# Loading batch 0's values for the global softmax behind the twelfth fetch of w_out, not behind the thirteenth

## The chip, the cores and the metric

The kernel runs on one core of a Trainium2 chip. The metric is the time of one execution on the device, in microseconds (us), as a median of runs. The profile is of one further execution, recorded by the hardware profiler.

## The reference, cut to what is computed

Local and global attention, then a dense feed-forward layer, then a soft mixture of experts, all in f32; `w_in` and `w_out` arrive as 64-bit integers.

```
x = attention(q_l, k_l, v_l, q_g, k_g, v_g)   # 4 batches x 8 heads; 512 local rows
                                              # (window +-32, and 32 global keys) and 32 global
                                              # rows that see all 544 keys and values
x = x.transpose(...).reshape(2176, 512)
h = x @ w_in;  g = max(0.01*h, h);  y = g @ w_out             # 512 -> 2048 -> 512
logits = y @ phi                                              # 32 slots, 8 experts x 4
slot_input = softmax(logits, over rows).T @ y
slot_out[e] = max(slot_input[e] @ w1[e], 0) @ w2[e]
out = softmax(logits, over slots) @ slot_out
```

## The kernel before

**Stages.** One core does all four batches. The first 60 us or so are the local attention of batch 0, in four pairs of heads: transposes of q and k (`a_T`, L390), scores of 32-row blocks against a window of 128 keys (`a_S`, tile `sc`, L434, with a maximum on VectorE at L446 and exponentials on ScalarE at L454), transposes of the weights (`a_E`, tile `etp`, L473), products with the values (`a_V`, tile `po`, L493). From then on the attention of a later batch is interleaved with the feed-forward layer of finished 128-row tiles: `b_X` (transpose of x, tile `xtp`, L659), `b_H` (x @ w_in in twelve matmuls of 128x512 for a 512-wide slice, tile `hp`, L689), `b_L` (transpose of g, `gtp`, L726) and the logits. The last 90 us are the experts, with two rounds of weights w1 and w2 (tile `ew`), and the output (`sop` L1297, `sp` L1307, `op` L1321, evicted at L1340 and stored at L1343).

**w_out.** `p_items` turns w_out into f32 while batch 0's rows go through `b_H`. A 128-row piece is fetched (`fetch`, L233), converted by two ScalarE passes (L250, L251), two VectorE passes (L253, L257) and one GpSimd pass (L261), stored to DRAM as `wo_f` for later (L338), transposed on TensorE (tile `wotp`, L345), evicted on ScalarE (tile `wt`, L347) and multiplied with phi (`prod`, tile `ptps`, L354). There are 20 fetches. `begin` issues the first twelve: eight half pieces into buffers borrowed from the attention (tiles `sraw`, `eraw`, `kraw`), then four whole pieces (tile `rraw`) that fill the ring of four buffers. The other eight follow one by one, each as a ring buffer is used up. `fetch` keeps its last DMA in `raw_last[0]`.

**The values for the global softmax.** The 32 global rows of a batch see all keys and values, so `g_V` (tile `gpo`, L579) needs the values of the whole batch at once: `load_vn(0)` loads them, 1 MB into the tile `vn` (L206) and 64 KB into `vg` (L211). Its only caller for batch 0 stands after twelve items of `p_items` have been run, of which the tenth half or whole piece has caused the thirteenth fetch. `tc.issue_after(ins)` puts the instructions of its block, on `ins`'s engine, behind `ins` in that engine's order; it adds no wait on `ins`'s completion.

**Order.** The program gives the items in order, but a list scheduler lays out each engine's instruction stream from them with modelled times and from priorities; on the chip each engine then runs its stream in that fixed order. All DMAs of this stretch are issued from SyncE's queue (SP) in its order: fetches, stores of `wo_f`, q and k of batch 1 (L162, tiles `qn`, `kn`), the values of batch 1's windows (tile `vw`: two loads L177 and one L180 into 32 partitions, then two copies L184 and one L185 that spread them over the other partitions).

Of the kernel before, what the change touches and what calls it, by code (L numbers as in the profile page):

```python
# [20 lines left out]
def kernel(  # L21
# [181 lines left out]
    def load_vn(b):  # L203
        t = sa.tile([P, NW + 2, 2, D], F32, tag="vw", name="vn", bufs=2)
        t = t.rearrange("p a c d -> p (a c d)").rearrange("p (h t d) -> p h t d", t=NT, h=H)
        nc.sync.dma_start(  # L206
            out=t.rearrange("p h t d -> p h (t d)"),
            in_=v_l[b].rearrange("h (p t) d -> p h (t d)", t=NT),
        )
        g = sa.tile([SG, H, D], F32, tag="vg", name="vg", bufs=1)  # L210
        nc.sync.dma_start(out=g, in_=v_g[b].rearrange("h k d -> k h d"))  # L211
        vnat[b] = (t, g)
# [13 lines left out]
    raw_last = [None]  # L226
# [89 lines left out]
    def p_items():  # L316
# [7 lines left out]
        def begin():  # L324
            with tc.issue_after(raw_last[0]):
                wout_s.spread([("se", 4)] * 4 + [("eT", 2)] * 2 + [("kw", 3)] * 2)
                wout_s.start()

        items.append((0.0, begin))

        wos = []
# [656 lines left out]
    def run(*items):  # L988
        for x in items:
            x[1]()  # L990
# [24 lines left out]
    with tc.issue_after(exp_last[0]):  # L1015
        conv(4)
        merge(hs[1], wit[:4])
        del wit[:4]
    pit = p_items()
    merge([(1, pit.pop(0)[1])] + hs[2], pit[:12])  # L1020
    del pit[:12]
    run(st2[2])
    run(st3[3])
    with tc.issue_after(raw_last[0]):
        load_vn(0)
    s4, s5, s6, s7 = (step(n) for n in range(NP, 2 * NP))
    h3 = [(2.6, lambda f=f: b_H(3, f)) for f in range(NQ)]
# [353 lines left out]
```

## Time and profile before

| what | us |
|---|---|
| median of 3 runs (499.71 to 501.77) | 499.89 |
| the profiled execution, its own time | 496.2 |
| its span, first to last instruction | 494.5 |
| TensorE (PE) busy in the span | 463.5 |
| VectorE (DVE) busy | 275.0 |
| ScalarE (ACT) busy | 234.3 |
| GpSimd (POOL) busy | 160.3 |

The profiled execution lies 3.7 us below the median of the runs, and 1.7 us of it lie outside the span. A share of the whole span says little here, since the stages have different limits: the stretch that the change touches is read by windows and by each engine's order of time.

### The profile page before, as it was taken

What the parts mean: (1) busy time and instruction counts of PE and PEld (TensorE: products, weight loads), DVE (VectorE), ACT (ScalarE), POOL (GpSimd) and SP (SyncE); (2) the same over time, 40 slices, a digit from 0 to 9 for tenths busy, and PEclk for the clock granted to TensorE, in tenths of its full rate; (3) what the DMA queues carried; (4) which work ended last, traced back from release to release, by engine and by line L of the source; (5) the groups of instructions that cost most, each with busy time, mean ns of one, the idle gap of its engine ahead of it and who ended that gap; (6) DMA issues with size and microseconds to landing.
All of it is one profiled execution on the core that took longest, in us unless ns stands there. A gap on an engine that the chain in (4) does not pass through costs nothing.

```text
span 494.5 us, 13438 instructions
## 1 busy us (share of the span) xinstructions
PE 463.5 (94%) x5323; PEld 322.0 (65%) x5323; DVE 275.0 (56%) x886; ACT 234.3 (47%) x680; POOL 160.3 (32%) x281
## 2 busy tenths in 40 slices
PE   7867889999989999999999999999999999999993
PEld 5645668666766657776777676777777777533463
DVE  4585888498547776556554656427666511413332
ACT  4776899588655345543435444234444432201122
POOL 2044887342400113460615243243667700000000
PEclk9986899999999999999999999999999999999998
DMA  9989598599457655334250231169420079999977
GB/s 177 223 200 267 183 292 313 185 304 311 150 143 144 143 118 93 85 76 129 60 106 1 60 60 45 44 220 405 150 78 2 23 266 357 364 397 371 305 237 214
DMA packets 118362, 90.23 MB, mean 182 GB/s; under 512 B 75356, under 2 KB 100764, under 8 KB 118300
## 3 DMA queue, kind: packets, MB, share of 16 engines
q1 hardware_dynamic: 115628, 88.33, 61.8%
q10 hardware_dynamic: 2672, 1.05, 0.8%
q8 instruction: 42, 0.69, 0.6%
q14 instruction: 20, 0.16, 0.1%
HBM read 76.68 MB, written 8.65 MB: 173 GB/s over the span
## 4 chain that ended last, share of the span: by engine, by line
PE 78%; DVE 4%; ACT 4%; DMA 1%; issue 1%; POOL 0%; ACTq 0%; DVEq 0%; POOLq 0%
PE hp L689 38%; PE gtp L726 4%; PE ehp L1221 3%; PE sc L434 3%; PE up L810 3%; PE po L493 3%; PE lg L740 2%; PE etp L473 2%; PE sop L1297 2%; PE sop L1275 1%; PE gpo L579 1%; PE wotp L345 1%; PE qTp L390 1%; PE kTp L390 1%; PE xtp L659 1%; PE gl L519 1%
## 5 line engine op out<-in xcount | busy, mean ns | idle before, releaser
L689 PE MATMUL hp<-wi,xxh 128*128 128x512 f32 x512 | 167.2, 408 | 1.2 <-ACT xxh L665 1.2
L689 PEld LDWEIGHTS hp<-wi,xxh 128*128 128x128 f32 x512 | 91.8, 190 | 28.2 <-issue 8.2
L717 POOL COPY g<-gb 32x256 f32<-32x256 f32 x206 | 82.7, 401 | 82.6 <-DVE gb L708 55.5
L689 PE MATMUL hp<-wi,xxl 128*128 128x512 f32 x256 | 101.0, 396 | 0.0
L696 ACT ACTIVATE g<-hp 128x512 f32<-128x512 f32 x60 | 35.3, 595 | 56.2 <-PE hp L689 54.2
L454 ACT ACTIVATE se<-se,nmx 128x128 f32<-128x128 f32 x128 | 49.6, 390 | 21.5 <-DVE nmx L452 21.4
L689 PEld LDWEIGHTS hp<-wi,xxl 128*128 128x128 f32 x256 | 48.3, 189 | 12.5 <-issue 1.7
L200 POOL COPY vw<-vw 32x1664 f32<-32x1664 f32 x10 | 15.8, 1575 | 78.3 <-DMA vw<-in_v_g_dram 34.9
L446 DVE CUSTOM_DVE_ANT_0 se<-sc,mask 128x128 f32<-128x128 f32 x128 | 28.9, 284 | 12.1 <-PE sc L434 12.0
L261 POOL TENSOR_TENSOR wn<-wn,rraw 128x512 int32<-128x512 int32 x16 | 22.8, 1435 | 34.5 <-DVE wn L257 33.0
L708 DVE STREAM_TRANSPOSE gb<-g 128x512 f32<-128x512 f32 x32 | 22.2, 702 | 19.3 <-ACT g L696 14.0
L434 PE MATMUL sc<-kw,qT 64*32 64x128 f32 x1024 | 29.2, 283 | 0.8 <-DVE mx L446 0.4
L493 PE MATMUL po<-vw,eT 128*32 128x64 f32 x1024 | 24.2, 232 | 3.5 <-issue 2.1
L261 POOL TENSOR_TENSOR wo<-wo,rraw 128x512 int32<-128x512 int32 x12 | 16.0, 1332 | 31.7 <-DVE wo L257 7.2
L434 PEld LDWEIGHTS sc<-kw,qT 64*32 64x32 f32 x1024 | 19.8, 109 | 8.9 <-issue 5.3
L493 PEld LDWEIGHTS po<-vw,eT 128*32 128x32 f32 x1024 | 18.4, 116 | 10.2 <-issue 7.4
L477 DVE COPY eT<-etp 128x512 f32<-128x512 f32 x28 | 18.7, 684 | 9.9 <-PE etp L473 9.9
L454 ACT ACTIVATION_READ_ACCUMULATOR se<-se,nmx 128x1 f32 x128 | 24.1, 188 | 0.0
L473 PE MATMUL etp<-identr,se 128*128 128x128 f32 x128 | 22.4, 296 | 0.2
L405 DVE COPY kw<-kT 128x672 f32<-128x672 f32 x32 | 19.8, 653 | 3.1 <-ACT kT L394 2.7
L251 ACT ACTIVATE rraw<-rraw 128x512 int32<-128x512 uint32 x28 | 18.7, 673 | 4.3 <-DMA rraw<-in_moe_w_out_dram 3.1
L473 PEld LDWEIGHTS etp<-identr,se 128*128 128x128 f32 x128 | 15.8, 146 | 6.3 <-ACT se L454 2.3
(232 smaller groups left out, 777.9 us busy)
## 6 DMA issues: line engine op xcount, KB each, us to landing
ew<-in_moe_w_dram SPq DMA_DIRECT2D x23, 1024.0 KB, 9.5
rraw<-in_moe_w_in_dram SPq DMA_DIRECT2D x16, 512.0 KB, 5.5
vw<-in_v_l_dram SPq DMA_DIRECT2D x60, 112.0 KB, 3.2
rraw<-in_moe_w_out_dram SPq DMA_DIRECT2D x12, 512.0 KB, 6.7
ew<-in_moe_w_dram SPq DMA_DIRECT2D x9, 512.0 KB, 9.2
ew<-in_moe_w_dram SPq DMA_DIRECT2D x17, 256.0 KB, 5.5
wo_f<-wo SPq DMA_DIRECT2D x16, 256.0 KB, 3.2
vn<-in_v_l_dram SPq DMA_DIRECT2D x4, 1024.0 KB, 6.3
```

The costliest lines, as they stand in the source:

```text
L261: nc.gpsimd.tensor_tensor(out=di, in0=di, in1=m, op=ALU.add)
L405: nc.vector.tensor_copy(kw[:, :, 0:96], src)
L434: last_a[0] = nc.tensor.matmul(bks[e][32 * u:32 * u + 32, P * T:P * T + P], qt[64 * e:64 * e + 64, 32 * U:32 * U + 32], kw[win(U) // (NW / ...
L446: nc.vector.tensor_tensor_reduce(out=s[:, T, :], in0=bk[:, P * T:P * T + P], in1=mask[:, 0 if T == 0 else 2 if T == NT - 1 else 1, :], sca ...
L454: exp_last[0] = nc.scalar.activation(out=s[:, T, :], in_=s[:, T, :], func=AF.Exp, bias=nmx[:, e, T:T + 1], accum_out=sm[:, T, e:e + 1],).ins
L473: last_a[0] = nc.tensor.transpose(pt[:, P * T:P * T + P], es[e][:, T, :], ident).ins
L493: last_a[0] = nc.tensor.matmul(pov[32 * u:32 * u + 32, T, e, :], ets[e][:, 32 * U:32 * U + 32], vw[:, win(U), e, :], start=True, stop=True ...
L689: nc.tensor.matmul(hp, a[:, k, :], w[c][:, k, :], start=(k == 0 and n == 0), stop=(k == KD - 1 and n == 2),)
L696: nc.scalar.activation(out=gs, in_=hp, func=AF.Prelu, alpha=0.01)
L708: nc.vector.transpose(out=gb[:, f % 2], in_=gs)
L717: copy(dst[32 * c:32 * c + 32, :, a], src[32 * a:32 * a + 32, :, c])
L726: nc.tensor.transpose(pt[:, P * c:P * c + P], g[:, o:o + P], ident)
```

## The change

`begin` appends the twelfth fetch's DMA to `raw_last` once the ring is full, and `load_vn(0)` is put behind that one instead of behind the fetch that was issued last when the line is reached, the thirteenth.

```
@@ -325,6 +325,7 @@
             with tc.issue_after(raw_last[0]):
                 wout_s.spread([("se", 4)] * 4 + [("eT", 2)] * 2 + [("kw", 3)] * 2)
                 wout_s.start()
+            raw_last.append(raw_last[0])
 
         items.append((0.0, begin))
 
@@ -1021,7 +1022,7 @@
     del pit[:12]
     run(st2[2])
     run(st3[3])
-    with tc.issue_after(raw_last[0]):
+    with tc.issue_after(raw_last[1]):
         load_vn(0)
     s4, s5, s6, s7 = (step(n) for n in range(NP, 2 * NP))
```

No instruction is added or taken away. The added line makes every later line's number one higher (L338 becomes L339). Because the scheduler's modelled times change with the load, the order of other instructions moves too, on TensorE between about 95 and 147 us of the profile and again in the last 25 us; GpSimd's order stays.

SP's queue at the first fetches of w_out, before (`wo_f` is the stored f32 copy):

```order
L233 DMA rraw<-in_moe_w_out_dram 128x1024 x4
L338 DMA wo_f<-wo 128x512 x5
L233 DMA rraw<-in_moe_w_out_dram 128x1024
L206 DMA vn<-in_v_l_dram 128x8x256
L211 DMA vg<-in_v_g_dram 32x8x64
L338 DMA wo_f<-wo 128x512
L162 DMA kn<-in_k_l_dram 128x4x64 x2
L162 DMA qn<-in_q_l_dram 128x4x64 x2
L233 DMA rraw<-in_moe_w_out_dram 128x1024
```

The same place in the changed kernel:

```order
L233 DMA rraw<-in_moe_w_out_dram 128x1024 x4
L206 DMA vn<-in_v_l_dram 128x8x256
L211 DMA vg<-in_v_g_dram 32x8x64
L339 DMA wo_f<-wo 128x512 x5
L233 DMA rraw<-in_moe_w_out_dram 128x1024
L162 DMA qn<-in_q_l_dram 128x4x64
L162 DMA kn<-in_k_l_dram 128x4x64 x2
L162 DMA qn<-in_q_l_dram 128x4x64
L339 DMA wo_f<-wo 128x512
```

The load of `vn` and `vg` moves ahead of five stores and the thirteenth fetch, and batch 1's second q and k move ahead of the sixth store.

ScalarE after the conversion of the thirteenth fetch, before (`rraw_1324`, `rraw_1353`, `rraw_1383` are fetches 14, 15 and 16):

```order
L250 ACTIVATE wo_1382<-rraw_1242 128x512
L347 COPY wt_1366<-wotp_1361 128x512
L594 COPY xg0_99<-gxt_1491 128x4x32
L394 ACTIVATE kT_1521<-kTp_1516 128x512
L251 ACTIVATE rraw_1324<-rraw_1324 128x512
L347 COPY wt_1366<-wotp_1391 128x512
L250 ACTIVATE wo_1432<-rraw_1324 128x512
L394 ACTIVATE qT_1528<-qTp_1523 128x512
L394 ACTIVATE kT_1638<-kTp_1633 128x512
L251 ACTIVATE rraw_1353<-rraw_1353 128x512
```

In the changed kernel:

```order
L250 ACTIVATE wo_1382<-rraw_1242 128x512
L251 ACTIVATE rraw_1324<-rraw_1324 128x512
L348 COPY wt_1366<-wotp_1361 128x512
L250 ACTIVATE wo_1432<-rraw_1324 128x512
L595 COPY xg0_99<-gxt_1491 128x4x32
L395 ACTIVATE kT_1521<-kTp_1516 128x512
L251 ACTIVATE rraw_1353<-rraw_1353 128x512
L348 COPY wt_1366<-wotp_1391 128x512
L395 ACTIVATE qT_1528<-qTp_1523 128x512
L395 ACTIVATE kT_1638<-kTp_1633 128x512
L250 ACTIVATE wo_1501<-rraw_1353 128x512
L348 COPY wt_1446<-wotp_1441 128x512
```

The first passes over fetches 14 and 15 move ahead of evictions that TensorE waits for.

TensorE at the scores and weight transposes of batch 1's second pair, before:

```order
L434 MATMUL sc0_1684<-kw_1650,qT_1645 32x128 x8
L473 MATMUL etp_1761<-identr_66,se_1599 128x128
L659 MATMUL xtp_1775<-identr_66,xn_462 128x128 x4
L473 MATMUL etp_1761<-identr_66,se_1599 128x128 x3
L354 MATMUL ptps_1659<-wt_1616,phis_152 32x128
L434 MATMUL sc1_1685<-kw_1647,qT_1645 32x128 x8
L434 MATMUL sc1_1685<-kw_1650,qT_1645 32x128 x8
L689 MATMUL hp_1791<-wi_464,xxh_1780 128x512
```

In the changed kernel:

```order
L435 MATMUL sc0_1684<-kw_1650,qT_1645 32x128 x8
L355 MATMUL ptps_1659<-wt_1616,phis_152 32x128
L494 MATMUL po_2116<-vw_1494,eT_1759 32x64 x4
L474 MATMUL etp_1761<-identr_66,se_1599 128x128
L660 MATMUL xtp_1775<-identr_66,xn_462 128x128 x4
L474 MATMUL etp_1761<-identr_66,se_1599 128x128
L346 MATMUL wotp_1627<-identr_66,wo_1542 128x128 x4
L474 MATMUL etp_1761<-identr_66,se_1599 128x128
L435 MATMUL sc1_1685<-kw_1647,qT_1645 32x128 x8
```

Four matmuls of `po`, which read the window values `vw_1494`, now stand ahead of the transposes and of the `hp` stream, where before they came after it. On SP the copies of `vw_1494` that they need (L184, L185) now follow the seventeenth fetch, where before two q loads and one k load stood between.

TensorE in the output stage, from the first store of results on, before:

```order
L1297 MATMUL sop<-ew,hzT 32x128 x3
L1321 MATMUL op<-sst,cT 128x256 x6
L1321 MATMUL op<-sst,cTg 128x256
L1297 MATMUL sop<-ew,hzT 32x128 x16
L1321 MATMUL op<-sst,cT 128x256 x2
L1297 MATMUL sop<-ew,hzT 32x128 x5
L1321 MATMUL op<-sst,cT 128x256 x2
L1297 MATMUL sop<-ew,hzT 32x128
```

In the changed kernel:

```order
L1298 MATMUL sop<-ew,hzT 32x128 x16
L1322 MATMUL op<-sst,cT 128x256 x6
L1322 MATMUL op<-sst,cTg 128x256
L1298 MATMUL sop<-ew,hzT 32x128 x16
L1322 MATMUL op<-sst,cT 128x256 x8
L1308 MATMUL sp<-so_6213,s_77 128x128
```

Thirteen matmuls of `sop` move ahead of the first `op`, and the later `op` are no longer mixed with single `sop`.

## Rows read from the trace of the kernel before

**Rows 1.** Windows: stretch, length, busy by engine, granted clock, DMA share, GB/s.

```profile
68.00:84.00 16.00, 16.00 (x87) 12.72 (x86) 14.77 (x24) 15.17 (x34) 12.59 (x11) 1.00 0.89 323
84.00:92.00 8.00, 8.00 (x43) 5.66 (x42) 3.00 (x8) 4.78 (x13) 3.82 (x5) 1.00 0.26 97
93.00:127.00 34.00, 32.28 (x417) 23.11 (x419) 27.88 (x85) 26.50 (x73) 10.80 (x8) 1.00 1.06 310
95.00:147.00 52.00, 48.47 (x699) 35.27 (x698) 35.73 (x114) 37.22 (x103) 14.69 (x11) 1.00 0.84 242
...
472.00:488.00 16.00, 14.37 (x185) 10.97 (x185) 6.96 (x14) 5.67 (x12) 0.00 (x0) 1.00 0.76 230
```

The engines of a row are, in this order, PE (TensorE's matmuls), PEld (its weight loads), DVE, ACT and POOL.

**Rows 2.** SP's queue in order of time: start, us of issuing, line, DMA.

```profile
73.11 4.23 SPq L233 DMA_DIRECT2D rraw<-in_moe_w_out_dram  x4
80.70 11.75 SPq L338 DMA_DIRECT2D wo_f<-wo  x5
92.55 0.37 SPq L233 DMA_DIRECT2D rraw<-in_moe_w_out_dram  x1
92.98 0.45 SPq L206 DMA_DIRECT2D vn<-in_v_l_dram  x1
...
99.87 0.47 SPq L233 DMA_DIRECT2D rraw<-in_moe_w_out_dram  x1
...
102.19 0.42 SPq L233 DMA_DIRECT2D rraw<-in_moe_w_out_dram  x1
...
109.36 1.26 SPq L162 DMA_DIRECT2D qn<-in_q_l_dram  x2
...
113.41 0.73 SPq L185 DMA_DIRECT2D vw<-vw  x1
```

**Rows 3.** DMA issues at 92.0, 99.8 and 112.6 us: size, us to landing.

```profile
vn<-in_v_l_dram SPq DMA_DIRECT2D x1, 1024.0 KB, 6.6
rraw<-in_moe_w_out_dram SPq DMA_DIRECT2D x1, 512.0 KB, 3.8
...
rraw<-in_moe_w_out_dram SPq DMA_DIRECT2D x1, 512.0 KB, 5.7
...
vw<-vw SPq DMA_DIRECT2D x1, 224.0 KB, 5.9
```

**Rows 4.** ScalarE in order of time; in brackets idle time before, and its releaser.

```profile
102.85 0.68 ACT L250 ACTIVATE wo<-rraw 128x512 f32<-128x512 f32 x1
...
108.24 0.71 ACT L251 ACTIVATE rraw<-rraw 128x512 int32<-128x512 uint32 x1
```

**Rows 5.** TensorE in order of time, the waits between 95 and 147 us.

```profile
98.32 1.06 PE L354 MATMUL ptps<-wt,phis 128*32 128x128 f32 x26 [0.17 <-ACT wt L347]
...
110.90 0.66 PE L345 MATMUL wotp<-identr,wo 128*128 128x128 f32 x4 [0.70 <-POOL wo L261]
...
114.94 1.08 PE L434 MATMUL sc<-kw,qT 64*32 64x128 f32 x32 [0.40 <-DVE mx L446]
...
138.69 1.06 PE L354 MATMUL ptps<-wt,phis 128*32 128x128 f32 x26 [0.34 <-ACT wt L347]
141.05 0.66 PE L726 MATMUL gtp<-identr,g 128*128 128x128 f32 x4 [1.30 <-DVE gT L728]
```

**Rows 6.** TensorE in order of time in the output stage.

```profile
473.56 0.98 PE L1321 MATMUL op<-sst,cT 128*128 128x256 f32 x6 [0.57 <-DVE sst L1311]
...
474.59 1.08 PE L1297 MATMUL sop<-ew,hzT 128*32 128x128 f32 x32
...
477.02 0.41 PE L1297 MATMUL sop<-ew,hzT 128*32 128x128 f32 x2
477.36 0.51 PE L1321 MATMUL op<-sst,cT 128*128 128x256 f32 x2
...
479.74 0.49 PE L1307 MATMUL sp<-so,s 128*128 128x128 f32 x2
```

**Rows 7.** DMA issues from 468.7 to 469.0: size, us to landing.

```profile
ew<-in_moe_w_dram SPq DMA_DIRECT2D x2, 256.0 KB, 5.3
```

More of the change, by code (lines that the diff above doesn't have):

```diff
@@ L327, in begin @@
                 wout_s.start()
+            raw_last.append(raw_last[0])
         items.append((0.0, begin))
@@ L1023 @@
     run(st3[3])
-    with tc.issue_after(raw_last[0]):
+    with tc.issue_after(raw_last[1]):
         load_vn(0)
```

## The prediction

> **What bounds the kernel now.** I read the windows first. In all the stretches that matter the granted clock is 1.00, and TensorE is the engine that is never far from full: 8.00 of 8.00 us before 92, and 48.47 of 52.00 from 95 to 147, where the order of instructions changes [rows 1]. ScalarE and VectorE have 37.22 and 35.73 of those 52. So a change of order here can give back at most the 3.53 us that TensorE idles in that stretch, and it can cost as much as its new order makes TensorE wait. The second thing to see is the DMA column. The load of `vn` is issued at 92.98 [rows 2], just as the queue fills up: from 93 to 127 the sixteen DMA engines are at 1.06, that is full, at 310 GB/s, while from 84 to 92 they are at 0.26 [rows 1]. The change takes 1.06 MB (`vn` and `vg`) out of the full stretch. TensorE's own order of time then shows which waits stand in the stretch: 0.17, 0.70, 0.40, 0.34 and 1.30 us, 2.91 together [rows 5]; the rest of the 3.53 is in pieces below 0.3 us each. In the output stage it idles 1.63 us of 16 [rows 1], 0.57 of it ahead of the first `op` [rows 6].
>
> **Part 1, the load itself, 77 to 93 us: 0.** The fetches of the ring are issued from 73.11 on over 4.23 us [rows 2], so `vn` would go out at about 77.4, 15.6 us earlier. At the 323 GB/s of that stretch [rows 1] its 1.06 MB take 3.3 us, and the five stores, issued from 80.70 on [rows 2], land up to that much later. Behind them are SP's next DMAs and the buffers of `wo`, which ScalarE must not write before a store has landed. ScalarE has 3.2 idle us in the 8 us after that (4.78 busy), GpSimd 4.2 and VectorE 5.0 [rows 1], and TensorE works on `hp` that needs none of it. I take 0; if the cover were gone, up to 3.3. The twelve fetches ahead are issued before `vn`: the thirteenth landed after 3.8 us although 1 MB of `vn` was issued 0.43 us behind it [rows 2, 3], so a later DMA takes little from an earlier one.
>
> **Part 2, 95 to 147 us, the waits that can go: -1.5.** The q and k of batch 1 go out ahead of the sixth store, and the fourteenth fetch follows about 1.5 us sooner than its 99.87 [rows 2], at an estimated 98.2, since SP does not stop for the store of a conversion first. The queue ahead of it is shorter by 1.06 MB, at 310 GB/s 3.4 us of DMA time. The conversions of fetches 14 and 15 stand earlier on ScalarE, so GpSimd's last pass comes earlier too: the 0.70 ahead of `wotp` goes. The `gpo` matmuls, whose values have landed long before, move into the 0.17 ahead of `ptps`; two groups of `gtp` transposes stand earlier, so the 1.30 for an eviction of `gtp` shrinks. All five waits gone would be -2.91 [rows 5], nothing gained 0. But the order before was also laid out without gaps by the scheduler's times, and the chip put 3.53 us of idle time into it; new waits will come up in the new order that I cannot see. I take half, -1.45, and write -1.5.
>
> **Part 3, a new wait on ScalarE: +0.4.** In the changed order ScalarE takes fetch 15's first pass six instructions after the conversion pass of 102.85 [rows 4], and not after nine. Six at about 0.45 us (0.68 for the longest there) make 105.6. The fetch is issued at an estimated 101.9 (before at 102.19 [rows 2]), so it would have to land within 3.7 us. Behind that pass stand the eviction `wt_1366` and the copies of q and k, which TensorE waits for. From below, the nearest row is the 3.8 us of fetch 13, which ran alone, so 0.1 us of waiting; from above the 5.7 of fetch 14 [rows 3], or the 6.05 within which fetch 15 was taken at 108.24 without a wait [rows 4], so 2.4. The queue ahead holds one store and fetch 14, less than in either full row; I take 4.1, a wait of 0.4.
>
> The Trainium skill (DMA: Bandwidth & Descriptors, section "Anatomy of one DMA") fits a DMA on GpSimd's path as 2.0 us plus its bytes over 436 GB/s. That is an estimated 3.2 us for 512 KB, and this part would be 0. The row of 3.8, the emptiest here, is already above it, so the trace decides against it and the term stays.
>
> **Part 4, the output stage: -0.6.** The first `op` now stands behind sixteen `sop` and not three. That covers the 0.57 of waiting for `sst`. It also lets the `op` run without single `sop` between them: mixed, an `op` takes 0.51 and a single `sop` 0.41, while in runs three `op` take 0.98 and sixteen `sop` 1.08 [rows 6], 0.33 and 0.07 each. Four `op` at 0.18 and four changes at 0.34 give 2.1 us. Against it, the fourth `sop` needs the last expert's weights, whose half is issued at about 468.8 and lands 5.3 us later [rows 7], at 474.1, where TensorE would be there at 472.8: 1.3 us of standing. So `sp`, before at 479.74 [rows 6], comes between 0.8 us later (no gain from runs, 1.3 instead of 0.57) and 1.4 earlier (-0.57 - 2.1 + 1.3). What follows is outputs through a queue that is 0.76 full [rows 1], which passes only part of it on. I take -0.6.
>
> **Sum.** 0 - 1.5 + 0.4 - 0.6 = -1.7 us. Against the profiled execution that is 494.5 for 496.2, a span of 492.8 for 494.5. The runs' median is 3.7 us above the profiled execution, for reasons outside the span that the change does not touch, so the forecast is 499.9 - 1.7 = 498.2. About 0.5%, 2.5 us, is what a measurement of this kernel can tell from no change.
>
> **Rivals.**
> *A stall at `po` (slower).* Four matmuls of `po` stand ahead of the whole `hp` stream. They read `vw_1494`, which is whole only when SP's copies L184 and L185 have landed. TensorE gets there about when it ended the scores after 114.94, without the 0.40 [rows 5]: 115.6. Before, the last copy was issued at 113.41 [rows 2], and such copies land 5.9 us later [rows 3], at 119.3. If that time stays, TensorE stands 3.7 us with ready work behind it, and the time is 499.9 - 1.7 + 3.7 = 501.9; with part 3 at its upper end 503.9. It decides from an issue later than 109.7 on. For it speaks that matmuls start in order: at 110.90 TensorE stood 0.70 us for one `wotp` while scores were queued behind it [rows 5]. Against it, the two q loads that hold SP at 109.36 for 1.26 us [rows 2] and one k load now stand behind the copies, so the last copy goes out about 2 us sooner and the queue is 3.4 us emptier. The Trainium skill (TensorE: Matmul & The Clock Gate, section "The mechanism") says the same of order: matmuls are strictly first in, first out. By that rule no later matmul can fill the gap.
> *No change.* ScalarE, not the DMA, sets the pace of the softmax between 104 and 120, so the waits only move, and the output stage is held by its DMAs: 499.9, within 0.8.
> *All of it.* All five waits go and the output stage gives its 1.4: 499.9 - 2.9 - 1.4 = 495.6, to 497.4 with 60% of it.
> *The change does not do what it says.* If `vn`'s buffer were not free at 77.4, SP would stand in front of five stores and a fetch and the conversion would stall. Its buffer held values of batch 0's second pair, whose `po` ended long before; at 92.98 SP issued it right behind the fetch [rows 2]. Each us of it costs up to one: 502 and more.
>
> **How the numbers follow.** The forecast, 497.2 to 499.2, gets 0.45; no change 0.22; all of it 0.16; the stall at `po` 0.13; the buffer 0.04. The forecast's lower edge puts 0.09 below 497.4, so faster is 0.25; of the stall and the buffer 0.15 lie above 502.4; same is 0.60. The range leaves out the outer half of "all of it" and the upper part of the stall: 496.2 to 502.0.
>
> **What would show it.** In the changed profile: `vn` issued near 77.4 and landed before 88, with TensorE still full to 92 (part 1); no 0.70 ahead of `wotp` near 110 and less than 3.5 us idle from 95 to 147 (part 2); a wait of ScalarE for `rraw` near 105.6 of under 1 us (part 3); `sop` waiting for `ew` near 473, `sp` before 479 (part 4). The prediction is wrong if TensorE stands at `po` near 115 for more than 2 us, or if its idle time from 95 to 147 grows.

## The result and the profile after

The changed kernel took a median of 503.22 us against 499.89, a ratio of 1.0074 [1.005, 1.0098]: by that ratio 3.7 us slower, where 1.7 us faster was forecast. On another chip, beside before: 500.71 against 497.69, 1.0086 [1.0053, 1.0119], by that ratio 4.3 us. (The medians themselves differ by less, 3.3 and 3.0 us.) All rows of after below are of that second measurement (the profile of the first fell into a disturbed execution); its span is 500.4 us, that of before beside it 495.3. The kernels measured from here on keep the line numbers of before (L338 is L338), but for one that says so.

The first view is again the windows, of after, in the stretches and columns of [rows 1]:

```profile
68.00:84.00 16.00, 16.00 (x87) 12.90 (x87) 13.00 (x22) 15.15 (x35) 12.39 (x11) 1.00 0.96 342
84.00:92.00 8.00, 8.00 (x42) 5.64 (x41) 2.64 (x10) 4.27 (x9) 1.61 (x3) 1.00 0.50 169
93.00:127.00 34.00, 30.23 (x404) 21.74 (x403) 26.31 (x80) 25.60 (x74) 12.70 (x10) 1.00 0.91 257
95.00:147.00 52.00, 46.94 (x651) 34.20 (x653) 36.81 (x114) 35.84 (x102) 14.68 (x12) 1.00 0.81 230
472.00:488.00 16.00, 13.55 (x224) 10.01 (x216) 6.18 (x13) 4.56 (x11) 0.00 (x0) 1.00 0.80 231
```

The load did leave the full stretch: the DMA share from 93 to 127 falls from 1.06 to 0.91. But TensorE idles 5.06 us from 95 to 147 instead of 3.53, at a granted clock of 1.00, and from 84 to 92, where it is still full, GpSimd has only 1.61 us of work instead of 3.82: the conversion chain stands in that window.

SP's queue of after in order of time, against [rows 2]:

```profile
73.31 4.70 SPq L233 DMA_DIRECT2D rraw<-in_moe_w_out_dram  x4
78.06 0.43 SPq L206 DMA_DIRECT2D vn<-in_v_l_dram  x1
78.54 2.34 SPq L211 DMA_DIRECT2D vg<-in_v_g_dram  x1
81.58 14.17 SPq L338 DMA_DIRECT2D wo_f<-wo  x5
95.85 0.37 SPq L233 DMA_DIRECT2D rraw<-in_moe_w_out_dram  x1
...
104.80 0.37 SPq L233 DMA_DIRECT2D rraw<-in_moe_w_out_dram  x1
...
113.56 0.73 SPq L185 DMA_DIRECT2D vw<-vw  x1
```

The load went out when foreseen, and the five stores follow almost as before; but they end at 95.75 instead of 92.45, and the thirteenth fetch goes out at 95.85 instead of 92.55.

**The ledger.** To see where the span grew, I cut it at six events that every trace shows: A from the first fetch that fills the ring (L233, 73 us) to the load of batch 1's values (L206, 166 us before), B from there to the first DMA of the experts' late weights (L1089, tile `ew`, 443 us before), C to the first `sp` on TensorE, D to the first `op`, E from the first store of outputs to the end (from `op` to that store it is 1.15 us, but 1.44 in e8).

| kernel | ratio to before [95%] | A | B | C | D | E |
|---|---|---|---|---|---|---|
| before, second profile | 0.9997 [0.9982, 1.0012] | 93.02 | 276.16 | 29.89 | 1.62 | 19.80 |
| after | 1.0086 [1.0053, 1.0119] | 95.97 | 277.45 | 28.77 | 3.75 | 19.98 |
| e1: after, two passes kept in place | 1.0028 [1.0001, 1.0056] | 92.71 | 276.25 | 29.89 | 1.62 | 19.94 |
| e2: after, four `sop` ahead of `op` | 1.0088 [1.0055, 1.0122] | 96.83 | 278.21 | 28.77 | 3.08 | 19.65 |
| e3: before, two passes moved | 1.0189 [1.0159, 1.0220] | 101.82 | 277.45 | 29.89 | 1.62 | 19.90 |
| e4: before, sixteen `sop` ahead of `op` | 1.0016 [0.9995, 1.0038] | 93.25 | 276.30 | 29.89 | 2.36 | 19.28 |
| e5: after, three `sop` ahead of `op` | 1.0065 [1.0036, 1.0093] | 95.25 | 278.43 | 28.77 | 1.62 | 19.83 |
| e7: load behind the first store | 1.0066 [1.0043, 1.0089] | 96.42 | 276.18 | 29.89 | 1.62 | 19.83 |
| e7: load behind the fourth store | 1.0012 [0.9992, 1.0032] | 94.22 | 276.33 | 29.89 | 1.62 | 19.82 |
| e8: after, one GpSimd copy as a DMA | 1.0048 [1.0030, 1.0066] | 102.01 | 276.30 | 28.77 | 4.23 | 19.49 |
| e9: before, one more DMA | 1.0003 [0.9987, 1.0018] | 93.42 | 276.22 | 29.89 | 1.62 | 19.94 |
| e10: e5 and e8 together | 1.0015 [0.9995, 1.0035] | 94.51 | 276.34 | 28.77 | 1.62 | 20.00 |
| e11: before, experts' matmuls grouped | 0.9988 [0.9964, 1.0011] | 94.38 | 276.12 | 27.20 | 2.85 | 21.50 |

After against before: A +2.95, B +1.29, C -1.12, D +2.13, E +0.18, and a start 0.39 earlier, +5.04 in all, the difference of the spans. Four stretches moved. The prediction had looked at two of them. All of it is of one execution each. The five profiles in which the order up to the experts is that of before (its first, with A of 92.76, and e0_before, e4, e9 and e11) have A between 92.76 and 94.38 and B between 276.12 and 276.30; C and D are the same to 0.01 us wherever their order is.

A starts at a DMA, and TensorE is not always equally far along there. The granted clock of e0_before from 65 to 70 us, ahead of the place of the change, in a window with the columns of [rows 1]:

```profile
65.00:70.00 5.00, 5.00 (x22) 4.01 (x22) 3.41 (x6) 3.48 (x7) 4.92 (x4) 1.00 0.95 275
```

The same window of after:

```profile
65.00:70.00 5.00, 5.00 (x16) 3.88 (x16) 3.87 (x6) 3.95 (x8) 4.47 (x4) 0.69 0.79 243
```

In after, TensorE ran part of this window at 1.2 GHz, after a wait of 1.84 us near 62. In the first profile of before the wait there is 1.92 us and the clock stays at 1.00, and e11, with the order of before, has 1.83 us and 0.66, so neither the order nor the length of the wait decides it. TensorE's first `wotp` then comes 9.41 us after the start of A and not 8.13. TensorE in order of time, before:

```profile
81.83 0.85 PE L345 MATMUL wotp<-identr,wo 128*128 128x128 f32 x4
```

After:

```profile
82.72 0.60 PE L345 MATMUL wotp<-identr,wo 128*128 128x128 f32 x4
```

So 1.28 of A's 2.95 us lie ahead of anything the load can do, and without them the two spans would differ by 3.8. Counted from this `wotp` to the end of A, the five profiles with the order of before agree within 0.5 us (84.61 to 85.07). Against e0_before's 84.89, after loses 1.67 us, e2 2.3, e5 0.7 and e10 0.9, all four with the same order here; e1 loses nothing, and the two e7 lose 3.5 (behind the first store, at a lower clock) and 1.3 (behind the fourth). These are the losses of the middle.

### The profile page after: what moved, and what is told of

Same layout as the page of the kernel before. It is cut to its first block, busy times and chain, and to the rows that moved or that the text cites. A ratio compares the mean times of both kernels' runs of the same rounds, so it can differ in the third digit from the quotient of the medians.

```text
span 859.0 us, 13436 instructions
## 1 busy us (share of the span) xinstructions
PE 846.6 (99%) x5323; PEld 485.6 (57%) x5323; DVE 273.7 (32%) x886; ACT 240.5 (28%) x680; POOL 158.3 (18%) x281
## 3 DMA queue, kind: packets, MB, share of 16 engines
q10 hardware_dynamic: 2672, 1.05, 0.5%
## 4 chain that ended last, share of the span: by engine, by line
PE 92%; ACT 1%; DVE 0%; issue 0%; DVEq 0%; ACTq 0%
PE hp L690 45%; PE ehp L1222 4%; PE gtp L727 4%; PE sc L435 4%; PE up L811 4%; PE po L494 3%; PE etp L474 3%; PE lg L741 3%; PE wotp L346 2%; PE sop L1298 2%; PE sop L1276 2%; PE xtp L660 2%; PE ptps L355 1%; PE op L1322 1%; PE qTp L391 1%; PE kTp L391 1%
## 5 line engine op out<-in xcount | busy, mean ns | idle before, releaser
L690 PE MATMUL hp<-wi,xxh 128*128 128x512 f32 x512 | 297.4, 688 | 0.9 <-ACT xxh L666 0.9
L690 PEld LDWEIGHTS hp<-wi,xxh 128*128 128x128 f32 x512 | 144.8, 295 | 85.2 <-issue 76.9
L690 PE MATMUL hp<-wi,xxl 128*128 128x512 f32 x256 | 173.6, 679 | 0.0
L690 PEld LDWEIGHTS hp<-wi,xxl 128*128 128x128 f32 x256 | 77.3, 302 | 42.5 <-issue 39.6
L435 PE MATMUL sc<-kw,qT 64*32 64x128 f32 x1024 | 48.3, 428 | 0.0
L200 POOL COPY vw<-vw 32x1664 f32<-32x1664 f32 x10 | 15.7, 1573 | 147.4 <-DMA vw<-in_v_g_dram 73.7
L1222 PE MATMUL ehp<-ew,siT 128*32 128x512 f32 x128 | 38.1, 1136 | 0.4 <-DVE siT L1212 0.4
L474 PE MATMUL etp<-identr,se 128*128 128x128 f32 x128 | 35.6, 437 | 0.0
L478 DVE COPY eT<-etp 128x512 f32<-128x512 f32 x28 | 19.3, 690 | 40.4 <-PE etp L474 40.3
L727 PE MATMUL gtp<-identr,g 128*128 128x128 f32 x112 | 29.7, 445 | 1.0 <-DVE gT L729 0.6
L811 PE MATMUL up<-g,d 128*32 128x512 f32 x120 | 29.9, 1087 | 0.3 <-DVE d L788 0.3
L727 PEld LDWEIGHTS gtp<-identr,g 128*128 128x128 f32 x112 | 18.3, 184 | 14.1 <-issue 8.7
```

Of the source, the lines that this page charges most:

```text
L435: last_a[0] = nc.tensor.matmul(bks[e][32 * u:32 * u + 32, P * T:P * T + P], qt[64 * e:64 * e + 64, 32 * U:32 * U + 32], kw[win(U) // (NW / ...
L474: last_a[0] = nc.tensor.transpose(pt[:, P * T:P * T + P], es[e][:, T, :], ident).ins
L690: nc.tensor.matmul(hp, a[:, k, :], w[c][:, k, :], start=(k == 0 and n == 0), stop=(k == KD - 1 and n == 2),)
L727: nc.tensor.transpose(pt[:, P * c:P * c + P], g[:, o:o + P], ident)
L811: ms["up"] = nc.tensor.matmul(up[32 * j:32 * j + 32, :], d, g[:, 512 * j:512 * j + 512], start=(n == 0), stop=(n == len(ds) - 1), skip_gro ...
L1222: nc.tensor.matmul(hp[n][32 * g:32 * g + 32, :], siT[:, k, :], w1x[k, n] if (r, g, k // 2) == (0, 3, 0) else w1t[4 * r + g, k // 2][:, k % ...
```

## The experiments

Two explanations stood against each other at first: that the loss is made in the middle, by the conversions delayed behind `vn`, or in the output stage, by the `sop` moved ahead of the first `op`. A third came out of the traces: VectorE held up by GpSimd near 247 us.

**The two kernels side by side, again** (no edit).

> The changed kernel itself, once more, for its profile beside the kernel before. Theory A (a stall in the middle, at `po` near 115 us or at a wait of ScalarE for a late fetch): TensorE's idle time from 95 to 147 us grows from 3.53 to 6 us or more, and the output stage idles about the 1.63 us of before. Theory B (the output stage): idle from 95 to 147 stays at 2 to 4 us, and the time from the end of the dense layer to the end of the span grows by 3 us or more. Theory C (the gain and the loss lie in neither): both stretches are within 1 us of before, and the 3.7 us lie between 147 and 440 us or in the granted clock.

> The kernel before, unchanged, on the same chip, for a second profile and for how far two profiles of one kernel differ: ratio 1.000 within 0.003, TensorE's idle time from 95 to 147 us within 0.5 of 3.53, the first `sp` within 0.7 of 479.74.

The loss repeats, and before against itself is 0.9997. None of the three theories holds by itself: TensorE's idle time grew to 5.06, short of A's 6, and each of the three places lost. This pair gives the rows for four findings.

*The conversion chain.* Of the DMAs issued between 79 and 90 us, the stores (count, size, us to landing), before:

```profile
wo_f<-wo SPq DMA_DIRECT2D x4, 256.0 KB, 2.0
```

After:

```profile
wo_f<-wo SPq DMA_DIRECT2D x3, 256.0 KB, 6.1
```

A store that took 2.0 us takes 6.1 behind `vn`. ScalarE's passes over the halves of a piece (`kraw`, L250) write the buffer that the first store reads. ScalarE in order of time, before:

```profile
86.35 0.74 ACT L250 ACTIVATE wo<-kraw 128x256 f32<-128x256 f32 x2
88.42 0.58 ACT L347 COPY wt<-wotp 128x512 f32<-128x512 f32 x1 [1.33 <-PE wotp L345]
```

After:

```profile
89.06 0.59 ACT L347 COPY wt<-wotp 128x512 f32<-128x512 f32 x1 [2.33 <-PE wotp L345]
89.54 0.78 ACT L250 ACTIVATE wo<-kraw 128x256 f32<-128x256 f32 x2
...
109.34 0.68 ACT L251 ACTIVATE rraw<-rraw 128x512 int32<-128x512 uint32 x1 [1.38 <-DMA rraw<-in_moe_w_out_dram]
109.92 0.56 ACT L347 COPY wt<-wotp 128x512 f32<-128x512 f32 x1
```

The passes come 3.2 us later. The scheduler put the copy `wt` ahead of them, a move that I had not read in the order:

```
+L347 COPY wt_1126<-wotp_1154 128x512
 L250 ACTIVATE wo_1160<-kraw_1085 128x256
 L250 ACTIVATE wo_1160<-kraw_1087 128x256
-L347 COPY wt_1126<-wotp_1154 128x512
```

From there the whole chain of fetches runs late, and at 109.34 ScalarE waits 1.38 us for fetch 15 with the next `wt` queued behind. TensorE's waits of after between 95 and 147 us, against [rows 5]:

```profile
100.95 1.06 PE L354 MATMUL ptps<-wt,phis 128*32 128x128 f32 x26 [0.43 <-ACT wt L347]
...
110.54 1.06 PE L354 MATMUL ptps<-wt,phis 128*32 128x128 f32 x26 [1.86 <-ACT wt L347]
...
114.83 1.08 PE L434 MATMUL sc<-kw,qT 64*32 64x128 f32 x32 [0.50 <-DVE mx L446]
...
120.71 0.30 PE L493 MATMUL po<-vw,eT 128*32 128x64 f32 x4 [0.82 <-DMA vw<-vw]
```

and, of the same view, the last two:

```profile
143.46 0.66 PE L726 MATMUL gtp<-identr,g 128*128 128x128 f32 x4 [0.55 <-ACT gT L728]
...
145.91 1.09 PE L726 MATMUL gtp<-identr,g 128*128 128x128 f32 x8 [0.74 <-DVE gT L728]
```

They are 4.90 us together, where [rows 5] have 2.91. The 0.70 and the 0.34 are gone, as foreseen; 1.86 and 0.82 are new. A wait for `wt` of 1.57 to 1.86 us near 110 stands in the profiles of after, e1, e2, e8 and e10, and two of 0.91 in e5's; these are the six kernels with the load right behind the twelfth fetch. None of the others has one of over 0.2 us there, the two e7 included.

*VectorE behind GpSimd.* VectorE in order of time, after:

```profile
246.98 1.47 DVE L452 TENSOR_SCALAR nmx<-mx 128x4 f32<-128x4 f32 x1
```

GpSimd beside it:

```profile
246.84 1.57 POOL L200 COPY vw<-vw 32x1664 f32<-32x1664 f32 x1
```

VectorE before:

```profile
244.43 0.15 DVE L452 TENSOR_SCALAR nmx<-mx 128x4 f32<-128x4 f32 x1
...
245.30 0.87 DVE L452 TENSOR_SCALAR nmx<-mx 128x4 f32<-128x4 f32 x1
```

GpSimd before:

```profile
244.57 1.58 POOL L200 COPY vw<-vw 32x1664 f32<-32x1664 f32 x1
```

An operation of 0.15 us stood until the copy ended: 246.98 + 1.47 is 248.45, 246.84 + 1.57 is 248.41. Before, the first of the pair slipped in 0.14 us ahead of the copy, and only the second was held, where nothing waited for it. After, the copy starts first, by 0.14. The evictions behind it come later, and TensorE stands at 252 us, where before it does not (no engine's order differs here, only who comes first):

```profile
252.74 0.66 PE L390 MATMUL qTp<-identr,qn 128*128 128x128 f32 x4 [1.02 <-ACT kT L394]
```

*The experts' hidden layer, second round.* TensorE in order of time, before:

```profile
446.51 2.76 PE L1221 MATMUL ehp<-ew,siT 128*32 128x512 f32 x18
...
449.79 1.05 PE L1221 MATMUL ehp<-ew,siT 128*32 128x512 f32 x2
```

After:

```profile
450.36 2.77 PE L1221 MATMUL ehp<-ew,siT 128*32 128x512 f32 x20
```

Two of twenty matmuls of the expert hidden layer (`ehp`) were alone before and cost 1.05 us; in a row with the rest they cost 0.01. (The program issues them in groups of four side by side: eighteen are four groups and a half, and the two fill the half.) That is nearly all of C's -1.12, a gain.

*The output stage.* TensorE of after in order of time:

```profile
475.49 0.70 PE L1307 MATMUL sp<-so,s 128*128 128x256 f32 x2 [0.54 <-DVE so L1303]
476.12 0.75 PE L1297 MATMUL sop<-ew,hzT 128*32 128x128 f32 x6
478.25 1.06 PE L1297 MATMUL sop<-ew,hzT 128*32 128x128 f32 x26 [1.39 <-DMA ew<-in_moe_w_dram]
479.25 0.97 PE L1321 MATMUL op<-sst,cT 128*128 128x256 f32 x6
```

Of before:

```profile
472.77 0.70 PE L1307 MATMUL sp<-so,s 128*128 128x256 f32 x2 [0.54 <-DVE so L1303]
...
474.39 0.98 PE L1321 MATMUL op<-sst,cT 128*128 128x256 f32 x6 [0.57 <-DVE sst L1311]
```

TensorE stands 1.39 us for the last expert's weights with the first `op` behind it, and the first `op` comes 3.75 us after `sp`, not 1.62. Column E says what that costs: in all rows but one the end follows the first store of outputs by 19.3 to 20.0 us.

**e1: the passes back in their place.** After, with the two first passes on `kraw` ahead of the copy `wt` (the copy of that chunk is issued behind them).

```
+    if (c, j) == (0, 1): late.append(lambda: nc.scalar.copy(wt, ps_t))
+    else: nc.scalar.copy(wt, ps_t)
...
+    with tc.issue_after(raw_first[0]):
+        [late.pop()() for _ in late[:]]
```

> The changed kernel with three instructions of ScalarE back in their old order: the two first passes on fetch 12's halves (`kraw`) ahead of the copy `wt` that waits for `wotp`. The new place of `vn` on SP and nearly all of the rest of the new order up to 147 us stay; the output stage comes out in the old order as a by-product. Theory M (these three instructions set the loss of the middle): the thirteenth fetch is issued near 93.3 and not 95.85, TensorE's idle time from 95 to 147 us falls from 5.06 to about 3.5, the loss up to 300 us falls from 3.7 to under 1, and the ratio to the kernel before is 0.998 to 1.002. Theory R (the rest of the new order or `vn`'s own traffic sets it): the loss of the middle stays at 2.5 to 3.7, only the 2 us of the output stage go, ratio 1.004 to 1.007.

1.0028, two thirds of the loss gone. ScalarE in order of time:

```profile
88.80 0.77 ACT L250 ACTIVATE wo<-kraw 128x256 f32<-128x256 f32 x2 [2.58 <-DMA wo_f<-wo]
```

The passes now wait 2.58 us for the store, in the open, and fetch 13 goes out at 95.35, half a microsecond ahead of after's. But the edit changed more than it meant to: the scheduler gave the middle a third order, and the output stage and the experts came out as before (C, D). So it does not separate the delay from the order. It does show that a delay of this size can be lived with in another order: A is 92.71, and the middle loses nothing although the wait near 110 is there (1.57 us) and TensorE idles 4.53 us from 95 to 147. The whole loss is 1.4 us (0.0028 of 497.6).

**e2 and e5: the output stage alone.** After, with fewer `sop` ahead of the first `op`: in e2 four remain, in e5 exactly three, as before.

```
e2: +with tc.issue_after(op_mm['first'] if (m, k // 4) == (1, 0) and k >= 1 else op_mm[m, k // 4]) if m else ExitStack():
e5: +with tc.issue_after(op_mm['first']) if (m, k // 4) == (1, 0) and 4 * k + g >= 3 else ExitStack():
         nc.tensor.matmul(
```

> The changed kernel with the old order of the output stage: thirteen of the sixteen `sop` stand behind the first `op` again; the middle stays as changed. Theory T (the end is set by the first output: from the first output DMA to the end of the span it took 19.8, 19.8 and 20.0 us in the three profiles, so sixteen `sop` ahead of the first `op` cost what they delay it): the first `op` comes 2 us sooner than 479.25, the second `sp` is not sooner than 482.33, and yet the time falls by about 2 us, ratio 1.004 to 1.005. If the order of the output stage gains what the prediction took (0.6), the time rises by that much, ratio 1.0095.

> The changed kernel with exactly three `sop` ahead of the first `op`, as before; in the run e2_out_order four stood there, and the fourth reads the last expert's weights, for which TensorE stood 1.39 us. Theory T (the end follows the first output by 19.3 to 20.0 us): the first `op` comes 1.6 us behind the first `sp`, near 477.1 and not 479.25, and the time falls by about 2 us, ratio 1.004 to 1.005. Theory W (the stream of the experts' weights sets the end, however the output stage is ordered): ratio 1.008 to 1.009 as before, the time from the first output to the end grows to 22.

e2 came out at 1.0088: the fourth `sop` already reads the last expert's weights, and TensorE stood 1.39 us all the same. With three, TensorE reads:

```profile
477.61 0.98 PE L1321 MATMUL op<-sst,cT 128*128 128x256 f32 x6 [0.56 <-DVE sst L1311]
```

D is back at 1.62, and the ratio falls from 1.0086 to 1.0065, about half of what theory T asked for, and their intervals overlap.

**e3 and e4: the two moves put into before.**

```
e3: +with tc.issue_after(pin[0]) if pin[1:] else ExitStack():    # pin[0]: the copy wt
         nc.scalar.activation(out=ds, ...
e4: +if (m, k) == (1, 4):
+    with tc.issue_after(last): ops(0, 0, 256, 256)
```

> The kernel before, `vn` in its old place, with only the two first passes on fetch 12's halves put behind the copy `wt` that waits for `wotp`; what the scheduler then moves stays as it comes out, the output stage is as before. Theory M: the passes run 2.5 to 3 us later, the thirteenth fetch is issued near 95.5 and not 92.55 to 93.60, the loss by 300 us is 2 to 3.5 us, ratio 1.004 to 1.007, without any move of `vn`. Theory R: within 0.002 of 1.

> The kernel before with one change: sixteen `sop` and not three stand ahead of the first `op` (after it, the order is nearly that of before). Theory T: TensorE stands for the last expert's weights, the first `op` comes 1.5 to 2.5 us later, the time from the first output DMA to the end stays at 19.8 to 20.0, ratio 1.003 to 1.005. The prediction's part 4: the second `sp` is 0.6 us sooner, at best 1.4, and the time falls by about that, ratio 0.997 to 0.999.

e3, 1.0189, cost far more than expected: the scheduler moved much else, and the granted clock was 0.88 from 120 to 147 us. It shows that a change of order alone can lose 9 us here, part of it by the clock, and says nothing on the size in question. e4 gave 1.0016, an interval that holds 1. The `op` stands behind sixteen `sop` there (its lines are L1300 for `op`, L1333 for `sop`):

```profile
474.75 1.06 PE L1333 MATMUL sop<-ew,hzT 128*32 128x128 f32 x26 [0.32 <-DMA ew<-in_moe_w_dram]
475.75 0.98 PE L1300 MATMUL op<-sst,cT 128*128 128x256 f32 x6
```

The weights are 0.32 us late here and not 1.39, so the first `op` slips by 0.74 only. The `sop` that wait for them start 31.25 us after the first DMA of the late weights here (443.50 to 474.75) and 31.52 in after (446.73 to 478.25); with C 1.12 shorter, TensorE is merely there sooner. The gain of C and the loss in D are in good part one and the same 1.1 us.

**e7: the load at another place of the queue.** After, with `vn` behind the first, or the fourth, of the five stores.

```
-    with tc.issue_after(raw_last[1]):
+    with tc.issue_after(st_ins[0]):      # in the other kernel st_ins[3]
         load_vn(0)
```

> The changed kernel with `vn` tied to the first store of `wo_f` and not to the twelfth fetch: one store is issued ahead of `vn`, four behind it. The output stage comes out in the old order. Theory S (the 1.06 MB of `vn` and `vg` delay the landing of the first store, and with it the buffer of `wo` into which ScalarE converts fetch 12's halves): ScalarE's wait of 2.3 to 2.6 us ahead of these passes goes, the thirteenth fetch is issued before 94.3 and not at 95.85, the loss by 152 us is under 0.7 and not 2.2 to 2.9, ratio 0.999 to 1.002. Theory R (the place of `vn` between 78 and 92 us does not matter, the new order behind it does): the thirteenth fetch moves, but the loss by 152 us stays at 2 us or more, ratio 1.004 or more.

> As the run e7_store1, with `vn` behind the fourth store: the instructions of TensorE, ScalarE and GpSimd stand in the same order as there. Theory S: the thirteenth fetch is issued near 93.6, the loss by 152 us is under 0.5, ratio 0.998 to 1.001. A dose rule (the more stores wait behind `vn`, the later the ring) would put this run below e7_store1 by 1 us or more; theory S puts the step at the first store, and the two runs within 0.5 us of each other.

This is the cleanest pair: the order of TensorE, ScalarE and GpSimd is the same in both, instruction by instruction (two rows of VectorE trade places), with the `kraw` passes ahead of `wt`; and B to E are as before. Only three stores more or less stand behind `vn`. 1.0066 against 1.0012, intervals apart: 2.7 us between two places in the queue, with the order held. Theory S, with its step at the first store, missed: fetch 13 went out early in both (94.28 and 93.07), and the first kernel still lost. Its loss does not look like idle time. Its windows:

```profile
95.00:120.00 25.00, 23.05 (x325) 15.51 (x323) 19.43 (x62) 18.64 (x48) 9.22 (x7) 0.89 0.96 271
120.00:147.00 27.00, 25.94 (x319) 19.78 (x318) 12.89 (x51) 17.90 (x53) 5.20 (x4) 0.92 0.67 191
```

TensorE idles 3.01 us of these 52, less than before, but the clock was granted at 0.89 and 0.92: from 116 to 124 us it was 0.50, that is 1.2 GHz. In the second kernel's profile it was 1.00 there, and TensorE idles 4.87. So this pair does not show a price of waiting: in the profiles the difference is the clock, and whether the place of the load brought it down is not shown. (The mean clock over the span is 0.961 to 0.973 in five runs of the first kernel, 0.964 to 0.980 in twelve of the second.)

**e9: bytes without a new order.** Before, with 0.66 MB more copied within DRAM, issued behind the twelfth fetch.

```
+    with tc.issue_after(raw_last[1]):
+        nc.sync.dma_start(out=dum, in_=v_l[0, 0:5])
```

> The kernel before, its order on every engine unchanged, with one DMA more on SP: 0.66 MB copied from one place of the memory to another, issued behind the twelfth fetch, where the change puts the 1.06 MB of `vn` and `vg`. Nothing waits for it. Theory S (bytes ahead of the stores delay their landing): the first stores land later than the 2.0 us of before, ScalarE stands up to 1.5 us ahead of its first pass on fetch 12's halves, and the thirteenth fetch is issued 0.3 to 1.5 us later; of that, 0 to 1.5 us arrive at 152 us, ratio 1.000 to 1.003. Theory R (only the new order matters): stores land after 2.0 us as before, no wait of ScalarE there, ratio within 0.001 of 1.

1.0003. ScalarE waits for the store, and nothing comes of it:

```profile
86.70 0.75 ACT L250 ACTIVATE wo<-kraw 128x256 f32<-128x256 f32 x2 [1.07 <-DMA wo_f<-wo]
```

So the cover of part 1 exists and holds for 1.07 us.

**e8 and e10: the copy that holds VectorE.** After, with the one GpSimd copy near 247 us (L200, twelfth window) done by a DMA on SP; e10 has e5's edit too.

```
-            nc.gpsimd.tensor_copy(t[96:128, 1:NW], ...)
+            (nc.sync.dma_start if n == 12 else nc.gpsimd.tensor_copy)(t[96:128, 1:NW], ...)
```

> The changed kernel with one instruction taken from GpSimd: the copy of `vw` that runs at 246.84 is made by a DMA; the order of everything else is that of the changed kernel. Theory P (a 4-column operation of VectorE that takes 0.15 us stood 1.47 us until that copy ended, and TensorE then stood 1.02 for the `kT` behind it): TensorE's 1.02 goes, the loss between 152 and 270 us falls from 1.1 to under 0.2, ratio 1.006 to 1.007. Theory N (ScalarE is late there for another reason): the loss between 152 and 270 us stays at 1 us or more, ratio 1.008 to 1.009.

> The changed kernel with three `sop` ahead of the first `op` (as e5_three_sop) and with the one copy of `vw` made by a DMA (as e8_no_copy). If the ledger holds (the middle to 152 us 1.6 to 3.3, the collision at 247 us 1.1, the output stage about 2), only the middle is left: the loss between 152 and 270 us is under 0.2, the first `op` comes 1.6 us behind the first `sp`, the span is 1.5 to 3 us above that of before, ratio 1.003 to 1.005. If the parts hide one another, the ratio stays at 1.0065.

TensorE's wait of 1.02 is gone in both, and B is 276.30 and 276.34. (The profiled execution of e8 took 507.17, where its median is 500.26: the clock was 0.82 and 0.79 from 95 to 147, so its A is not comparable.) With after and e5 they make a square:

| ratio to before | `sop` as the change puts them | three `sop` first, as before |
|---|---|---|
| GpSimd copy | 1.0086 | 1.0065 |
| copy by DMA | 1.0048 | 1.0015 |

The copy is worth 0.0038 or 0.0050, 1.9 or 2.5 us, more than the 1.1 that the profile of after shows in B; the place of the `sop` 0.0021 or 0.0033, 1.0 or 1.6 us. What stays, 1.0015, is 0.7 us, within the interval of nothing. If C's gain of 1.1 from the profile is in it, the middle still loses some 1.8. By the intervals each of the four differences is uncertain by 1.3 to 2.2 us: the cost of the copy is clearly above zero, that of the place of the `sop` barely, and the four kernels ran on three chips, each beside before. The stop itself, with TensorE's wait of 1.00 to 1.05 behind it, is in the profiles of after, e2, e5 and e3; e1, both e7 and all with the order of before have the copy but not this stop. The four that stop are also profiles with the low clock from 65 to 70, so whether the order of after brings it in every execution is open. That the runs give more than the 1.1 may be since other copies collide too, in some kernels: e5, whose B is 278.43, has a second stop. VectorE of e5:

```profile
185.49 1.61 DVE L406 COPY kw<-kgT 128x224 f32<-128x224 f32 x1
```

GpSimd of e5 at the same time:

```profile
185.37 1.57 POOL L200 COPY vw<-vw 32x1664 f32<-32x1664 f32 x1 [17.80 <-DMA kn<-in_k_l_dram]
```

TensorE waits 0.90 us for VectorE at 187 there, and has no such wait in after or in e10.

**e11: the gain of stage C, alone.** What was still open was whether the -1.12 is one of order alone and can be had without the load's move. Before, with the lone `ehp` held behind the row.

```
+with tc.issue_after(sop_ins) if r and (n or k >= 2) else ExitStack():
     nc.tensor.matmul(
```

> The kernel before, `vn` in its old place; the only change: the `ehp` matmuls of the experts' second half that stand alone between transposes and `sop` (2, 4, 1 and 1 records, which took 1.05, 1.05, 0.62 and 0.59 us) are held behind the last `sop` of the first half, so that the four experts' matmuls stand side by side again. Theory G (a single `ehp` of 32 columns' rows costs about as much as four side by side, and the 1.13 us that the changed kernel won back between 443 us and the first `sp` is one such pair moved into its row: 18 records in 2.76 us before, 20 in 2.77 after): the first `sp` comes 1 to 2.5 us sooner than in the kernel before, the first output with it, the time from the first output to the end stays at 19.3 to 20.0, ratio 0.995 to 0.998. Theory D (the experts' weights, not TensorE's order, set the first `sp`): waits for `ew` take the place, ratio 0.999 to 1.001.

C falls to 27.20, and the end does not follow: 0.9988 [0.9964, 1.0011], no proven gain. TensorE of e11 in order of time:

```profile
474.21 0.41 PE L1297 MATMUL sop<-ew,hzT 128*32 128x128 f32 x2 [1.47 <-DMA ew<-in_moe_w_dram]
```

Windows of e11:

```profile
474.00:490.00 16.00, 14.64 (x176) 11.30 (x177) 6.07 (x12) 4.80 (x10) 0.00 (x0) 0.89 0.73 227
```

The same window of before:

```profile
474.00:490.00 16.00, 13.38 (x177) 10.59 (x177) 6.87 (x14) 5.97 (x12) 0.00 (x0) 0.98 0.79 239
```

Part of the time won is spent waiting for the last weights (1.47), and the clock behind that wait was 0.89 where before has 0.98; E is 21.50 in this profile, 1.7 longer.

## Why the prediction was wrong, step by step

**Part 1, "I take 0; if the cover were gone, up to 3.3", is the step that failed first.** The delay was sized about right: a store took 4.1 us longer, fetch 13 went out 3.3 later than in the first profile of before, or 1.6 later counted from TensorE's first `wotp`. The cover was not. I counted idle time of ScalarE, GpSimd and VectorE within the next 8 us, and TensorE's full window; both stood (8.00 of 8.00). But the chain fetch, conversion, store, fetch is serial, and its delay comes out a turn later: 1.38 on ScalarE at 109, 1.86 on TensorE at 110, and a wait of this kind near 110 in all six kernels with the load right behind the twelfth fetch. e9 shows the cover: 1.07 us of delay cost nothing. What the waits cost in the end is less sure: the middle lost 0.7 to 2.3 us in four profiles of this order, and nothing in e1, which has the delay in another order. The twelve fetches ahead were indeed not slowed: ScalarE waited 0.26 us for the last, 0.22 before.

**Part 2, -1.5, had the wrong sign.** The waits of 0.70 and 0.34 went; fetch 14 left at 99.74, not 98.2, and fetch 15 at 104.80, not 101.9, as both estimates rested on part 1's 0. Idle time grew by 1.5, which the prediction had named as its own refutation. How much of the middle's loss is the delay itself and how much the order that the scheduler made of it stays open: e1 has the early load and loses nothing there, the second e7 has fetch 13 nearly as early as before and loses 1.3, and e3 has the late load and loses 7.3, a low clock included.

**Part 3, +0.4, was the right mechanism at the wrong size:** 1.38 on ScalarE, 1.86 on TensorE. The fetch landed within 4.5 us of its issue (104.80 to 109.3), near the 4.1 taken; it left 2.9 us later than assumed, and 1.6 later than in the profile of before beside it.

**Part 4, -0.6, had the wrong sign for the end.** TensorE did what was worked out: from the first `sp` to the second it needs 6.84 us instead of 7.79 (before 472.77 to 480.56, after 475.49 to 482.33), 0.95 less, within the range given. The step "passes only part of it on" failed: none is passed on, as the first `op` is 2.13 later and the end follows the first store. By runs it cost 1.0 to 1.6 us, with an uncertainty of 1.3 to 2.2. The wait for the weights, 1.3, was foreseen to 0.1; it was charged to the second `sp` instead of to the first `op`.

**What no part had:** the stop of VectorE near 247, 1.9 to 2.5 us by runs, and the grouped `ehp`, -1.12. I had compared the orders between 95 and 147 us and in the last 25, not in between, where the `ehp` moved. The stop of VectorE would not have shown in any order: it comes from a shift of some 0.3 us between two engines.

**Rivals.** The stall at `po` came, at 0.82 us rather than 3.7: the last copy left at 113.56, but TensorE, itself late, only reached `po` at 119.9. "Slower" had been given a rival, but it came about for a reason that none of the rivals had. That the runs' median lay 3.7 us above the profiled execution "for reasons outside the span" was also misread: in the runs on record a time exceeds its span by 1.7 to 2.1 us, so most of it lay within the span. Nothing in the sum hangs on it.

By these sizes the sum reads: middle +1.8 instead of -1.1, VectorE +2.2, experts -1.1, output +1.3 instead of -0.6, 4.2 us in all; measured were 3.7 and, on the second chip, 4.3 (0.0086 of 497.69). That the sum meets the 4.3 proves nothing: three of its terms are taken from the same square of runs, the middle as what is left over. What speaks for the middle by itself are the 0.7 to 2.3 us of the profiles.

## What to carry to other kernels

A bulk load put ahead of write-backs whose buffers are reused delays the serial loop through these buffers, and a full TensorE in the next few microseconds doesn't show that it is free: follow the chain for one whole turn. When a scheduler lays out the order, compare every engine's stream from start to end, and then look in the trace for waits far behind the change too: here one came up 170 us after the load, where no order had changed. Before a stretch is compared between two profiles, see whether the engines enter it at the same point and at the same clock. In a last stage that drains through a full DMA queue, count to the first store, not to the middle of TensorE's work.

## What the runs showed of the hardware

**VectorE stands for a whole GpSimd instruction.** Here 1.47 us for an operation of 0.15, decided by 0.14 us in who starts first. In ten traces of these kernels, 17 to 22 operations of VectorE take over 0.5 us longer than the quick ones of their line and shape, and every one of them ends 0.02 to 0.55 us after a GpSimd operation ends: 0.03 for operations of 0.15 us, 0.15 for those of 0.28, 0.42 for copies of 0.54, 0.55 for those of 0.68 (the one of e5 above 0.16 after, 187.10 against 186.94). The longer the operation is by itself, the later behind GpSimd's end it ends, so nearly all of its work seems to be done after that end. The Trainium skill (SBUF — State Buffer, section "Who interferes with whom") says that the two share one pair of ports, which, when VectorE is in one of its two-port modes, the first to start holds for its whole instruction while the other is fully blocked, and names `tensor_scalar` among those that can enter such a mode. The traces agree, by the ends above and by e8 and e10, where the wait goes with the copy.

**The drain is nearly constant.** From the first store of outputs to the end it is 19.3 to 20.0 us in twelve of the thirteen rows of the ledger, whatever TensorE did in between; the thirteenth, e11, has 21.5 and a lower clock there; from 488 to 496 us of after the DMA engines are 0.99 busy.

**A lone pair of `ehp` matmuls** (weights of 128x32, 512 columns) costs 1.05 us, and 0.01 where it fills the last group of four in a row of twenty.

**The clock can give way in these stretches.** In e3, e7 (behind the first store) and e11 the granted clock was 0.88 to 0.92 where before has 0.98 to 1.00, in streams of the same matmuls, and 0.69 against 1.00 from 65 to 70 us in after, where the two programs still have the same order. At 1.2 GHz two `hp` matmuls take 1.05 us there, at 2.4 GHz 0.63. One profile of each does not tell whether an order brings it about; what does was not tried.
